# Two spectral-filter and MLP layers on one core: contiguous copies behind the d transform, a table half by DMA, and new instruction orders

## The chip, the core and the metric

The kernel runs on one core of a Trainium2 chip. The metric is the device time of one execution in microseconds (us). Of the kernel before there are three timed runs, with a median of 349.98 us (349.18 to 350.13), and one profiled execution, which took 349.9 us and whose instructions span 348.0 us. Positions in time below are microseconds from the start of that span.

## The reference

Two pairs of sublayers act on x, 2048 rows of 512 values in bf16 (2D transforms over both axes in FP32):

```python
x = x + irfft2(rfft2(layernorm(x)) * (w_r + 1j * w_i))      # A, a spectral filter
x = x + B(layernorm(x))                                     # B, an MLP with shifted rows
x = x + irfft2(rfft2(layernorm(x)) * (w_r + 1j * w_i))
x = x + B(layernorm(x))
```

B computes `h = gelu(layernorm(x) @ w1)`, shifts the four column quarters of h by -1, +1, -2 and +2 rows, multiplies by w2 and adds x (giving x1), and then returns `x1 + gelu(layernorm(x1) @ w3) @ w4`, with 1792 columns between w3 and w4. Both layers use the same weights.

## The kernel before

**Data.** x stays in SBUF as `K.x`, 128 partitions by 16 row slots q by 512 columns. Row number is 16p + q, so the transform over the 2048 rows splits into one over p (a matmul over the partitions) and one over q with twiddle factors.

**The stages of a layer**, with the letter that stands for each piece of work in the order strings:

- The first norm and the p transform. `s`, `i` and `J` compute mean and reciprocal deviation of a row slot; `Q` multiplies the table T of cosines and sines with the reciprocal deviation (`scaled_T`, L371 to L378, on DVE or ACT), and `O` is the matmul of x with that scaled table (L389, L391). So the norm costs no pass over x. `G` copies the products from PSUM to V (`take_V`, L416). In layer 1 this is `first_front` with the string ORDER_0; slots 1 and 5 have their sums made by ACT, and `FILL` puts two or three dummy matmuls behind some products. In layer 2 it is spread through the end of layer 1's MLP.
- The d transform: `d` (L504, matmuls with the table FA), then `t`, which copies its product from PSUM to a bf16 tile TV (`take_d`, L508 to L516). A unit is one or two blocks b of 128 rows of V, so a copy has 512 or 1024 columns. In layer 1 the copy permutes two halves h into alternate places; in layer 2 it is plain, since there the weights W have been permuted instead (`L`, L751).
- The q transform: `q` (L528, with the tables TL), `x` copies to X (L534), `p` multiplies X with W on DVE (`weigh`, L547). `b` is the q transform backwards (L558, with TR), `m` copies to hT (L569). The table TR has three planes, of which the third is the negated first.
- `D` and `P`: d and p transforms backwards (L576, L588); `Y` copies between them; `a` adds into x (L596).
- The MLP: `s`, `r`, `n` a norm, `T` a transposing DMA, `v` and `h` w1 and gelu, `u` w2 (L644), `f` and `E` the residuals, `k`, `R`, `o`, `U` the second norm and its transposes, `w` and `g` w3 and gelu (L679, L686), `W` w4 (L699, 14 matmuls of 512 columns), `A` the last residual (L705), `y` the store (L708). In layer 1, `W14` and `W24` are the two column halves of one row slot's product (`columns`, L688).

**What sets the order.** Nothing is scheduled at run time: ORDER_0, ORDER_A (layer 1) and ORDER_B (layer 2) list the work, each engine takes its own part of the list in that order, and waits for other engines arise from the data. A last letter V or A puts a copy on DVE or ACT, and a number behind a point names the PSUM bank. `X4.6` is four dummy matmuls. `WAKE` (L788) is the number of dummy matmuls at the very start.

**Loads.** SP's queue loads x in eight pieces and W in 16. POOL's queue (`load_rest`, L179) loads FA, TL and the first half of TR, and then, in this order, doubles W onto the odd partitions in four DMAs from SBUF to SBUF and makes the second plane of TL by two instructions for each half (`turn_TL`, L227: L230 and L231), then loads the second half of TR:

```python
double(0)
turn_TL(K, slice(0, 8))
double(1)
turn_TL(K, slice(8, 16))
double(2)
double(3)
load_TR(1)
```

`load_TR` fetches planes 0 and 1. The negated plane is made by DVE in two halves, `N0` and `N1` (`negate`, L759, L762). A DMA on SP (`gate2`, L201) reads W's last doubled row, so G, Tinv and w1 to w4, which stand behind it on SP, start when the doubling is done.

## Time and profile before

| | us | of the span of 348.0 |
|---|---|---|
| PE matmuls, 2129 | 339.1 | 97% |
| DVE | 185.6 | 53% |
| ACT | 197.2 | 57% |
| POOL | 61.8 | 18% |
| w3 products, L679, 448 | 99.8 | |
| w4 products, L699, 462 | 99.3 | |
| dummy matmuls, L254, 67 | 11.3 | |

Busy time of PE is the union of its matmuls, each counted from its start to its modelled end; they overlap, and 14 matmuls of 512 columns in a row take 3.02 us, 0.216 each, although each one's own duration is shown as 379 ns. The distance between two starts is therefore what counts in a row of matmuls, and dummy matmuls count as busy. The same holds on DVE and ACT in a smaller way: a following instruction starts up to 0.1 us before the one ahead of it ends, so a row of instructions takes less than the sum of their durations. A line of a group names line, engine, operation, what is written and read, and the shape, then total busy time, mean duration in ns, and the idle time of the engine just ahead of it with what ended it.

The first product of scaled tables starts at 8.46, the first d at 19.12, the first D at 39.18, the first v at 53.73, the first w at 82.16; in layer 2 the first d at 184.90, the first D at 204.57 and the first v at 219.24. The last matmul starts at about 343.7, the last add runs from 343.89 to 344.58, and its store lands at 346.38.

### The profile page before, as it was taken

To read this page: it belongs to the slowest core of one execution; us is meant where nothing else is said; L and a number is where in the kernel's file an instruction comes from. 1 tells how busy PE (TensorE), PEld (TensorE's weight loads), DVE (VectorE), ACT (ScalarE), POOL (GpSimd) and SP (SyncE) were. 2 spreads that over 40 slices of the span, in tenths; PEclk is the share of its full clock that TensorE was granted. 3 is DMA by queue.
4 is the path that set the end of the run, shared out by engine and by line. 5 is a ranking of instruction groups with operands and counts; after the bars stand their busy time and mean duration, and the time that the engine had idled before them with its cause. 6 is when DMAs were issued, how large, how long until landed. Compare 5 with 4: busy or idle time off the path is not lost. (4 is left out here: it accounts for less than half of the span.)

```text
span 348.0 us, 5581 instructions
## 1 busy us (share of the span) xinstructions
PE 339.1 (97%) x2129; PEld 189.3 (54%) x2129; DVE 185.6 (53%) x444; ACT 197.2 (57%) x350; POOL 61.8 (18%) x157
## 2 busy tenths in 40 slices
PE   8899999999999999999999999999999999999995
PEld 6778885444444444445577888544444444444442
DVE  5989596559424317844786969767343201102011
ACT  5979899754803706424528989985580372150410
POOL 2560055422200003200100002463130010000000
PEclk9999999999999999999999999999999999999999
DMA  7987935304030110400000002454003400400201
GB/s 240 319 326 238 377 82 115 75 13 57 1 62 0 30 33 0 90 2 0 1 2 0 2 2 44 80 107 76 0 2 60 90 0 16 107 0 17 75 0 60
DMA packets 45129, 24.38 MB, mean 70 GB/s; under 512 B 34928, under 2 KB 42096, under 8 KB 45104
## 3 DMA queue, kind: packets, MB, share of 16 engines
q1 hardware_dynamic: 43760, 20.00, 23.3%
q0 software_dynamic: 1104, 3.94, 3.0%
q8 instruction: 16, 0.26, 0.3%
q10 hardware_dynamic: 240, 0.10, 0.1%
q14 instruction: 9, 0.07, 0.1%
HBM read 11.41 MB, written 2.10 MB: 39 GB/s over the span
## 5 line engine op out<-in xcount | busy, mean ns | idle before, releaser
L686 ACT ACTIVATE gT<-ps 128x1024 bf16<-128x1024 f32 x56 | 56.4, 1022 | 103.6 <-PE ps L679 103.2
L679 PE MATMUL ps<-xT,w 128*128 128x512 bf16 x448 | 99.8, 379 | 0.5 <-DMA xT<-xn 0.5
L699 PE MATMUL ps<-w,gT 128*128 128x512 bf16 (+1 forms) x462 | 99.3, 373 | 0.0
L705 DVE TENSOR_TENSOR x_state<-ps,x_state 128x512 bf16<-128x512 f32 (+1 forms) x33 | 22.0, 674 | 98.0 <-PE ps L699 98.0
L699 PEld LDWEIGHTS <-gT 128*128 128x128 bf16 x462 | 45.1, 98 | 51.3
L679 PEld LDWEIGHTS <-w 128*128 128x128 bf16 x448 | 43.7, 98 | 53.1 <-DMA xT<-xn 0.9
L652 DVE SCALAR_TENSOR_TENSOR xn<-xn,ln_c,ps 128x512 bf16<-128x512 bf16 x32 | 23.3, 744 | 25.0 <-PE ps L644 9.3
L644 PE MATMUL ps<-w,hT 128*128 128x512 bf16 x128 | 29.3, 379 | 0.0
L628 PE MATMUL ps<-xT,w 128*128 128x512 bf16 x128 | 28.7, 379 | 0.0
L596 DVE SCALAR_TENSOR_TENSOR x_state<-ps,x_state 128x512 bf16<-128x512 f32 x32 | 20.4, 685 | 7.1 <-PE ps L588 7.0
L282 ACT ACTIVATE junk<-xn 128x512 bf16<-128x512 bf16 x32 | 19.9, 622 | 5.9 <-DVE xn L652 5.7
L270 DVE BATCH_NORM_STATS2 ln_st<-x_state 128x6 f32<-128x512 bf16 (+1 forms) x31 | 20.1, 667 | 3.5 <-DMA x_state<-in_A_x_dram 3.2
L644 PEld LDWEIGHTS <-hT 128*128 128x128 bf16 x128 | 12.4, 98 | 15.4 <-ACT hT L635 0.4
L628 PEld LDWEIGHTS <-w 128*128 128x128 bf16 x128 | 12.4, 98 | 14.9 <-issue 0.7
L282 ACT ACTIVATE xn<-x_state 128x512 bf16<-128x512 bf16 x32 | 20.0, 630 | 0.4
L547 DVE TENSOR_TENSOR PB<-X,W 128x2048 bf16<-128x2048 bf16 (+1 forms) x20 | 19.4, 1009 | 0.5 <-ACT X L151 0.4
L635 ACT ACTIVATE hT<-ps 128x512 bf16<-128x512 f32 x32 | 17.6, 605 | 3.2 <-PE ps L628 2.9
L288 POOL TENSOR_SCALAR ln_mv<-ln_s 128x4 f32<-128x4 f32 x16 | 4.3, 268 | 77.4 <-DVE x_state L596 66.7
L151 ACT ACTIVATE TV<-ps 128x1024 bf16<-128x1024 f32 (+1 forms) x15 | 14.3, 980 | 3.4 <-PE ps L504 2.1
L504 PE MATMUL ps<-FA,V 128*128 128x256 bf16 x128 | 16.0, 273 | 0.2 <-ACT V L151 0.2
L576 PE MATMUL ps<-G,hT 128*128 128x256 bf16 x128 | 15.3, 273 | 0.8 <-ACT hT L151 0.4
L305 POOL TENSOR_SCALAR ln_ve<-ln_mv 128x4 f32<-128x4 f32 x11 | 3.3, 298 | 71.8 <-DVE ln_mv L298 71.1
(86 smaller groups left out, 393.6 us busy)
## 6 DMA issues: line engine op xcount, KB each, us to landing
w<-in_B_w_dram SPq DMA_DIRECT2D x2, 1792.0 KB, 12.2
W<-W POOLq DMA_DIRECT2D x4, 514.0 KB, 4.7
x_state<-in_A_x_dram SPq DMA_DIRECT2D x8, 256.0 KB, 5.5
out_dram<-x_state SPq DMA_DIRECT2D x16, 128.0 KB, 1.9
TR<-tab_TR POOLq DMA_DIRECT2D x2, 512.0 KB, 6.4
w<-in_B_w_dram SPq DMA_DIRECT2D x2, 512.0 KB, 4.6
W<-in_A_w_r_dram SPq DMA_DIRECT2D x7, 128.5 KB, 6.1
W<-in_A_w_i_dram SPq DMA_DIRECT2D x7, 128.5 KB, 6.0
```

The lines of the kernel that those rows point to most:

```text
L270: self.K.nc.vector.bn_stats(self.st[i][:, int(k)], src)
L282: K.nc.scalar.activation(out, src, ACT.Square, bias=0.0, scale=D ** -0.5, accum_out=self.s[:, i, 1:2])
L547: nc.vector.tensor_tensor(t, X.pop(u)[:, 0:2 * n].unsqueeze(1).to_broadcast([P, 2, 2 * n, 256]), K.W[:, :, 2 * u:2 * u + 2 * n, 1:257], op ...
L596: nc.vector.scalar_tensor_tensor(K.x[:, q, :], ps.pop(("P", q)), 1.0, K.x[:, q, :], op0=ALU.mult, op1=ALU.add, accum_out=ln[g].s[:, i, 0:1])
L628: nc.tensor.matmul(o[:, i], lhsT=K.w1[:, t, j * P:(j + 1) * P], rhs=xT[g][:, :, t, :], start=(t == 0), stop=(t == 3))
L635: nc.scalar.activation(hv[:, 2 * h + i, 4 * g:4 * g + 4, PAD:PAD + P], o[:, i].rearrange("p (q c) -> p q c", q=4), ACT.Gelu_apprx_tanh, bi ...
L644: nc.tensor.matmul(o, lhsT=K.hT[:, j, st:st + P], rhs=K.w2[:, j, :], start=(j == 0), stop=(j == 3))
L652: nc.vector.scalar_tensor_tensor(xn[:, q, :], xn[:, q, :], ln[q // 4].c[:, q % 4:q % 4 + 1], ps.pop(("u", n)), op0=ALU.mult, op1=ALU.add, ...
L679: nc.tensor.matmul(o[:, i], lhsT=K.w3[:, c, t * P:(t + 1) * P], rhs=xT3[g][:, :, c, :], start=(c == 0), stop=(c == 3))
L686: nc.scalar.activation(gT[g][:, 2 * j:2 * j + 2, :], ps.pop(("w", k)), ACT.Gelu_apprx_tanh, bias=0.0, scale=1.0)
L699: nc.tensor.matmul(o, lhsT=gT[g][:, t, i * P:(i + 1) * P], rhs=K.w4[:, t, d], start=(t == 0), stop=(t == 13))
L705: nc.vector.tensor_tensor(x, ps.pop(("W", n)), x, op=ALU.add)
```

## The change

- `take_d` in layer 1 writes TV contiguously and reads PSUM with the two halves h innermost: consecutive elements lie 128 FP32 apart, in pairs. The same values go to the same places as before; only the order in which the copy walks over them differs.
- The table TR in DRAM gets its negated plane. The first half is loaded as before, two planes, with `N0` making the third on DVE; the second half is loaded with all three planes, and `N1` is gone.
- Behind the first doubling of W, POOL copies two values of the last scaled table of the first norm into a tile `gate` that nobody reads, and so waits for that table there.
- 35 dummy matmuls at the start instead of 44.
- In layer 2 row slot 10 of the list is made in two column halves (`W10`, `W20`), each with its own add and its own store, as row 14 was in layer 1 (where this stays).
- All three orders are new. ORDER_0 begins with rows 0 and 1 and puts Q0, Q1 and Q9 on DVE, Q8 on ACT. In layer 1 the TV copies on ACT are 0, 1, 4, 8, 10, 12 and 15 (before 1, 2, 8, 10 and 12), and of the hT copies 1, 2, 3, 6, 7 and 9 are on DVE (before 0, 1, 8 and 9), half of 15 in both. In layer 2 the TV copies 1, 8 and 15 go to DVE, where ACT made all before, and x4 goes to ACT. Counts of matmuls, copies and products are otherwise as they were.

The diff, with the long orders cut to their starts, layer 1's first MLP part and their ends:

```diff
--- before.py
+++ after.py
@@ -88,6 +88,7 @@
     Bt = B.transpose(0, 1, 3, 2)
     TR = np.stack([np.stack([At, Bt], axis=3), np.stack([Bt, -At], axis=3)], axis=2)
     TR = TR.reshape(NH, 2, 2, 32, 2, 64).transpose(3, 2, 1, 4, 0, 5).reshape(P, 2, NH, 64)
+    TR = np.concatenate([TR, -TR[:, :1]], axis=1)
     out = {"T": np.stack([T, -T], axis=1), "FA": FA, "TL": TL, "TR": TR, "G": G, "G2": G2,
            "Tinv": np.stack([T.T, -T.T], axis=1)}
     return {k: np.ascontiguousarray(v.astype(ml_dtypes.bfloat16)) for k, v in out.items()}
@@ -176,16 +177,18 @@
     K.TL = K.const.tile([P, 2, NB, P], BF16, name="TL")
     K.TR = K.const.tile([P, 3, NH, 64], BF16, name="TR")
 
-    def load_rest():
+    def load_rest(after):
         q = nc.gpsimd
         load_TL = lambda k: q.dma_start(K.TL[:, 0, 8 * k:8 * k + 8], dram["TL"][:, 8 * k:8 * k + 8])
-        load_TR = lambda k: q.dma_start(K.TR[:, 0:2, 16 * k:16 * k + 16], dram["TR"][:, :, 16 * k:16 * k + 16])
+        load_TR = lambda k: q.dma_start(K.TR[:, 0:2 + k, 16 * k:16 * k + 16], dram["TR"][:, 0:2 + k, 16 * k:16 * k + 16])
         double = lambda k: q.dma_start(K.W[1::2, :, 8 * k:8 * k + 8], K.W[0::2, :, 8 * k:8 * k + 8])
         table("FA", q)
         load_TL(0)
         load_TL(1)
         load_TR(0)
         double(0)
+        gate = K.const.tile([1, 2], BF16, name="gate")
+        q.tensor_copy(gate[:], after[0:1, 0, 0:2])
         turn_TL(K, slice(0, 8))
         double(1)
         turn_TL(K, slice(8, 16))
@@ -438,6 +441,8 @@
             L[g].sums()
     ps = {}
 
+    last_T = None
+
     def stats(q):
         g, i = at[q]
         if q in ON_ACT:
@@ -451,8 +456,10 @@
         L[g].aggr(i)
 
     def scale(q, eng):
+        nonlocal last_T
         g, i = at[q]
         scaled_T(K, q, L[g].r[:, i:i + 1], eng)
+        last_T = K.Tq[q]
 
     def front(k):
         ps[k] = over_p(K, FIRST[k], k == len(FIRST) - 1)
@@ -474,7 +481,7 @@
             table[op[0]](int(op[1:-1]), op[-1])
         else:
             table[op[0]](int(op[1:]))
-    K.load_rest()
+    K.load_rest(last_T[:])
     K.load_mlp()
     spare = K.grp.tile([P, 4, 4, P], BF16, name="xT", bufs=4)
     K.nc.sync.dma_start_transpose(spare[:, 0, 0:1], K.zeros[:])
@@ -512,8 +519,8 @@
         if last:
             copy(K, tv[u][:], src, eng)
         else:
-            copy(K, tv[u][:].rearrange("p n (e f h) -> p (n e) h f", e=2, h=2),
-                 src.rearrange("p n (e h f) -> p (n e) h f", e=2, h=2), eng)
+            copy(K, tv[u][:].rearrange("p n (e f h) -> p (n e) f h", e=2, h=2),
+                 src.rearrange("p n (e h f) -> p (n e) f h", e=2, h=2), eng)
 
     def over_q(u):
         bs = UNITS[u]
@@ -687,9 +694,9 @@
 
     def columns(n):
 
-        if last or n % 10 != 4 or n < 14:
+        if n not in (HALVES[last], HALVES[last] + 10):
             return n, slice(0, D)
-        return 14, slice(0, D // 2) if n == 14 else slice(D // 2, D)
+        return HALVES[last], slice(0, D // 2) if n == HALVES[last] else slice(D // 2, D)
 
     def w4(n):
         r, d = columns(n)
@@ -705,7 +712,8 @@
         nc.vector.tensor_tensor(x, ps.pop(("W", n)), x, op=ALU.add)
 
     def store(n):
-        nc.sync.dma_start(K.out_v[:, ROWS[n], :], K.x[:, ROWS[n], :])
+        r, d = columns(n)
+        nc.sync.dma_start(K.out_v[:, ROWS[r], d], K.x[:, ROWS[r], d])
 
     def stats4(n):
         r, d = columns(n)
@@ -785,13 +793,14 @@
             table[op[0]](int(op[1:]))
 
 
-WAKE = 44
+WAKE = 35
 FILL = {0: 3, 1: 3, 2: 2, 3: 2, 4: 2}
 GROUPS = [[0, 1, 2, 3], [4, 5, 6, 7], [8, 9, 10, 11], [12, 13], [14, 15]]
 ON_ACT = [1, 5]
 FIRST = [[0, 1], [2, 3], [4, 5], [6, 7], [8, 9], [10, 11], [12, 13], [14], [15]]
 UNITS = {b: [b, b + 1] if 2 <= b < 14 else [b] for b in (0, 1, 2, 4, 6, 8, 10, 12, 14, 15)}
 ROOT = (0, 1)
+HALVES = (14, 10)
 LATE = ((14, 15), (0, 14))
 TAKE_B = ("FFFFFFFFFFFFFFFB", "FFFFFFFFFFFFFFFB")
 ROWS = [*range(2, 16), 0, 1]
@@ -799,46 +808,46 @@
 PLAIN = 5
 FLEX = "mGnotxY"
 ORDER_0 = """
-s0 s2 s3 i0 i2 i3 s1 f0 S0 s4 J0 Q2V Q3V O1 i4 s5 s7 s6 Q1A Q0A i7 i6 G1A f1 S1 O0 G0A s11 s10 i11 J1 Q6A i10 s8 s9
-Q7A Q4A i8 i9 s13 Q5A s12 S2 J2 i13 i12 Q10V O3 G3A Q11A O2 Q8V O5 Q9A s15 s14 S3 J3 i15 i14 G2A S4 Q13V Q12V J4 Q14V
-G5A Q15A O4 O6 G6A G4V O7 G7V O8 G8A G8V
+s0 s2 i0 s3 s1 i2 i3 f0 s4 S0 J0 i4 s5 Q1V Q0V Q3V Q2V s7 s6 i7 i6 s9 s11 O0 G0A f1 i9 S1 J1 s8 O1 G1A Q6A s10 Q7A i11
+O3 i8 i10 Q5A s13 s12 Q4A O2 S2 J2 i13 Q10V G3A i12 Q9V s15 Q11A O5 S3 Q8A s14 i15 G2A O4 i14 S4 J3 Q12V G5A J4 Q15A
+Q13V O6 Q14V G6A G4V O7 G7V O8 G8V G8A
 """
 ORDER_A = """
-N0 X4.6 d0.5 t0V d1.7 t1A d2.2 t2A q0.0 x0V p0 q1.6 d4.4 d10.0 q2.2 x1A t10A p1 t4V d6.6 t6V q4.4 x2A x4A p2 p4 d12.1
-t12A q10.6 q6.3 d14.0 d8.1 t14V x6A p6 x10A b0.3 t8A b3.5 b2.6 m2A b5.4 b1.0 p10 m3A m1V m0V m5A q8.1 x8A q12.6 N1
-d15.5 t15V b6.0 b4.3 b7.2 x12A q15.6 m4A p8 p12 q14.4 m6A x14A b10.3 b9.0 m10A m9V b11.1 m7A x15A p14 p15 m11A b8.4
-b12.5 m12A b13.0 m13A m8V b14.1 m14A b15.6 m15V m15A D1.3 Y1A D0.0 Y0A D3.5 Y3A P2.3 a2 s2 P3.1 P0.0 a3 s3 a0 s0 P1.2
...
-T1 v0.6 r2 v1.3 s15 c2 h0 a13 h1 T2 a12 n9V T3 v3.5 s12 n8V T4 h3 n11V v2.3 u0.0 h2 s13 u1.4 n10V s14 r3 c3 u3.5 f1 T5
-k1 v5.3 h5 f3 k3 v4.1 h4 f0 n15V n13V n12V u2.7 n14V f2 T6 k0 u6.6 f6 u4.1 E1 E2 k2 k6 f4 T7 u7.4 u5.0 f5 v7.1 h7 R0
-E3 o3A f7 v6.0 u8.3 f8 o2V h6 u11.4 o1A E4 u9.0 u15.5 E0 o0V f15 u13.3 k8 f9 f13 k9 f11 u10.1 k5 L15 E7 E5 k4 u12.2 E6
-k7 R1 U1 f10 k11 o6V f12 u14.3 U0 L13 w3.4 w6.6 g6 L4 w1.1 g1 g3 o5V f14 k10 w0.6 w2.0 g2 g0 L12 w5.2 g5 o7V o4A E8
...
-W12.7 L7 j11 j9 O3.5 W15.4 j8 A12 B12 G3A G3V A15 B15 S2 Q10 z0 j15 S15 Q8 J15 j12 W13.2 Q15 W24.5 Q9 W14.3 A13 B13
-j13 S13 S12 Q11 A24 J13 Q13 O4.0 G4A J12 B24 Q12 A14 B14 j14 S14 O15.6 G15V G15A J14 Q14 O5.4 G5A O6.2 G4V O14.6 G14V
-G6A G14A X4.5 X3.4 L6
+X4.1 N0 d0.3 t0A d2.5 d1.7 t1A d4.0 t4A q0.2 x0A t2V q1.4 x1V p1 d10.6 d6.4 p0 t6V q2.1 t10A q4.6 x2A p2 x4A d12.3
+b1.0 q6.1 p4 q10.6 t12A m1V b3.3 m3V x6A d8.4 d14.2 d15.0 x10A b5.6 t8A q8.4 p6 t14V t15A q12.0 b2.7 p10 m2V q14.2 m5A
+x8A x12A q15.4 b0.6 m0A b10.7 m10A b4.1 m4A p8 b6.0 p12 m6V x14A p14 b11.7 x15A b9.1 p15 b13.6 m11A m9V m13A b7.3
+b12.5 m12A b8.2 m8A b14.7 m14A m7V b15.5 m15A m15V D1.1 Y1V D0.5 D3.3 P2.7 a2 P3.2 a3 Y0A P0.1 a0 Y3A P7.4 P1.7 a1 s2
...
+L0 v0.1 h0 a12 a13 v1.5 h1 T3 r2 c2 v3.4 n11V s12 c0 n10V T5 n8V n9V h3 s15 v2.3 h2 u0.5 L8 u3.0 u2.7 f0 L2 s14 f3
+u1.5 f1 s13 r3 n12V n14V n15V f2 T4 v5.2 n13V h5 v4.1 u4.5 f4 E1 h4 u7.6 u6.1 f7 E3 u5.4 T7 k1 k0 f6 f5 k3 k2 E5 R0 c3
+T6 v7.5 h7 u15.7 E0 v6.0 h6 E6 E4 u8.4 k7 o0V k5 o1V f15 E2 k6 o2V u10.3 o3V f10 k10 u12.7 u11.0 f8 u14.1 f14 U0 U1
+u9.2 f9 k9 k8 w2.4 g2 f12 L9 E9 k4 R1 f11 k11 R2 w5.6 E11 g5 w4.2 g4 w1.0 u13.4 E8 o8V g1 o9V w3.5 g3 f13 E10 o10V
...
+Q10 G1V g27 W12.5 A12 O3.0 B12 W15.6 j12 Q5 G3A G3V A15 O2.2 G2A B15 Q8 j15 G2V S15 J15 Q15 W13.5 A13 B13 S12 W24.4
+A24 j13 S13 J12 Q12 B24 J13 W14.5 Q13 A14 B14 O4.0 G4A O15.2 j14 S14 O5.6 G15V G15A O6.4 J14 Q14 O14.2 G4V G5A X3.7
+G14V L6 G6A X4.1 G14A
 """
 ORDER_B = """
-d4.0 d1.3 d8.6 t4A q4.0 t1A q1.2 t8A x4V d15.5 t15A p4 d12.6 x1A p1 t12A d10.4 q15.0 x15A p15 t10A q8.2 x8V q12.6 x12A
-d2.0 t2A d0.4 d14.5 b1.3 m1A q10.0 t0A q2.6 t14A p8 b8.3 x2A m8A d6.4 t6A p12 x10V b5.2 m5A p2 b12.1 m12A p10 b13.0
-q0.4 m13V q6.6 x0A x6A q14.2 b4.1 m4A p0 b10.4 b11.5 p6 x14A m11A m10A b3.6 m3A b9.0 b0.1 m0A p14 m9V b7.2 m7V b2.7
...
-W5.0 A5 y13 w20.5 W7.4 g20 w14.2 g14 A7 w15.4 y4 g15 w16.0 g16 w18.5 g18 W9.2 A9 y7 W8.3 A8 W11.4 y15 A11 W10.7 A10 y5
-y6 y14 y11 y9 y8 y10
+d1.1 d4.3 t1V d15.7 t15V d8.0 t8V t4A q1.2 x1A p1 q4.6 x4A p4 d12.4 q15.2 t12A d10.6 x15A p15 t10A q8.0 q12.4 x12A
+b1.2 m1A d14.6 d2.3 t14A x8V p12 t2A d0.0 t0A b5.2 m5A p8 q10.5 x10V p10 q2.3 x2A d6.0 t6A b9.2 p2 b4.3 m9A q0.4 x0A
+p0 q14.6 m4A x14A q6.0 x6A b13.2 b12.4 m12A b10.3 b0.7 m0A p14 b3.5 m3A b2.0 m13A m10V p6 b14.3 b11.4 m2V b8.6 m11A
...
+W6.4 A6 w14.0 w15.3 g15 W5.2 g14 w18.0 A4 A5 g18 w17.6 g17 y7 y5 y6 w19.4 g19 W9.2 A9 W10.5 y4 y9 A10 y10 W8.0 A8
+W11.4 W20.6 A11 A20 y8 y14 y11 y20 z0
 """
```

## The prediction

> **What bounds the kernel now.** I read the page's busy shares first: PE is busy for 97% of the span, so a gain must come from places where PE runs dummy matmuls, waits, or has ended. To find them I cut the span at the borders of the stages:
>
> ```profile
> core 0: us, PE busy (x) PEld busy (x) DVE busy (x) ACT busy (x) POOL busy (x), PEclk, DMA share, GB/s
> 1.01:8.46 7.45, 7.45 (x44) 5.66 (x45) 4.24 (x13) 5.05 (x13) 1.73 (x9) 1.00 0.85 267
> 8.46:19.12 10.66, 9.35 (x82) 7.58 (x79) 10.27 (x31) 9.62 (x19) 5.97 (x8) 1.00 1.00 334
> 19.12:39.18 20.06, 19.50 (x256) 15.88 (x257) 18.38 (x24) 18.08 (x26) 4.65 (x6) 1.00 0.85 298
> ...
> 82.16:184.90 102.74, 102.51 (x533) 50.36 (x533) 56.42 (x144) 43.60 (x63) 10.92 (x22) 1.00 0.09 19
> 184.90:204.57 19.67, 19.00 (x256) 16.31 (x257) 16.53 (x20) 18.22 (x29) 0.00 (x0) 1.00 0.01 2
> ...
> 219.24:343.87 124.63, 124.61 (x578) 56.09 (x575) 38.26 (x96) 54.29 (x95) 19.96 (x52) 1.00 0.20 46
> 343.87:348.00 4.13, 0.00 (x0) 0.00 (x0) 0.69 (x1) 0.00 (x0) 0.00 (x0) 0.97 0.10 33
> ```
>
> The two long stretches after 82.16 and 219.24 are matmul back to back; nothing can be won there. The stretch to 8.46 is 44 dummies. From 8.46 to 19.12 DVE is busy for 10.27 of 10.66 us: the first norm is bound by DVE. The spectral stage of layer 1 (19.12 to 39.18) has 256 matmuls. PE's timeline starts 64 of them 0.109 us apart (d), 64 in pairs at 0.055 each (q), 128 at 0.056 (b), so PE needs 17.6 of 20.06 us, while DVE (18.38) and ACT (18.08) are nearly full. That stage is bound by copies, in layer 1 with dearer ones than in layer 2. First ACT in layer 1 (window 18.6 to 39.5), then the same group in layer 2 (184 to 206):
>
> ```profile
> L151 ACT ACTIVATE X<-ps 128x1024 bf16<-128x1024 f32 x6 | 5.9, 1048 | 0.0
> L151 ACT ACTIVATE TV<-ps 128x1024 bf16<-128x1024 f32 x4 | 5.3, 1328 | 0.8 <-PE ps L504 0.6
> ```
>
> ```profile
> L151 ACT ACTIVATE TV<-ps 128x1024 bf16<-128x1024 f32 x6 | 6.2, 1035 | 1.2 <-issue 1.2
> ```
>
> Layer 1's copy writes every second bf16 and costs 1.328 us; layer 2's, contiguous, 1.035. On DVE in layer 1:
>
> ```profile
> L149 DVE CAST TV<-ps 128x1024 bf16<-128x1024 f32 x2 | 2.6, 1308 | 0.2 <-PE ps L504 0.2
> L149 DVE CAST TV<-ps 128x512 bf16<-128x512 f32 x3 | 2.2, 735 | 0.2 <-PE ps L504 0.2
> L762 DVE TENSOR_SCALAR TR<-TR 128x1024 bf16<-128x1024 bf16 x2 | 0.9, 457 | 0.0
> ```
>
> DVE's contiguous cast of that size (X in layer 2) takes 1.222. PE's own waits are short, so a small loss is enough to make new ones:
>
> ```profile
> PE ps L389 <- DMA W<-in_A_w_i_dram: 1.2, 1, 1.2
> ...
> PE ps L679 <- DMA xT<-xn: 0.5, 1, 0.5
> PE ps L576 <- ACT hT L151: 0.4, 1, 0.4
> ```
>
> The first (at 11 to 12.2) is really a wait for a scaled table of ACT: Q6A starts at 11.66 and O3 at 12.21, and O3 reads no W. Last, DVE's timeline where the first norm meets POOL's turning of TL, which begins at 15.67:
>
> ```profile
> 13.80 0.47 DVE L376 TENSOR_SCALAR Tq<-T,ln_r 128x256 bf16<-128x256 bf16 x2
> ...
> 15.73 0.82 DVE L376 TENSOR_SCALAR Tq<-T,ln_r 128x256 bf16<-128x256 bf16 x2
> ```
>
> The same two instructions take 0.47 us alone and 0.82 beside POOL.
>
> [...]The new read takes each element [...](neighbours 512 bytes apart); the trace shows no such read, so this stays a risk. Against it: take_V jumps after every four elements[...] and still costs 1.02 us for 1024 on ACT. On SBUF writes [...]a step of 4 bytes costs 28% on ACT.
>
> **The change part by part.**
>
> *First norm (ORDER_0, WAKE, gate).* Nine dummies fewer: the last of them run 0.109 us apart, so they end at 8.46 - 0.98 = 7.48. Q1 and Q0 now stand on DVE ahead of Q3 and Q2, so O0 can start when DVE has done them, about 7.6. This is not the gain: the end of the stage is DVE's. DVE takes two scaled tables more (2 x 0.19 start to start, +0.38) and ACT two fewer. The gate puts POOL's turning behind the last scaled table: Q12/Q13 go back to 0.47 (-0.35) and Q14 (0.59 at 16.82) to 0.27 (-0.3). DVE's idle pieces before J1 (0.22), s4 (0.19) and Q14 (0.1) shrink by some 0.2. Sum -0.45: the first d at about 18.7 instead of 19.12. What the gate queues behind it on POOL: two turns (1.66 + 0.77, 1.79 + 0.75), three doublings of W and TR's second half. From a gate at 16.6 the first turn ends at 19.2 (q0 reads it at 21.4), the second at 22.5 (q10 reads it at 26.7). The last doubling waited for W until 23.51 before and still does, so SP's gate2 with G, Tinv and w1 to w4 behind it keeps its time: cost 0.
>
> *Negation by DMA.* N1 goes: one DVE instruction, 0.42 (0.33 start to start). TR's second half grows from 512 to 768 KB. It was issued at 24.12 and landed at 29.44; 256 KB at the stage's 298 GB/s are 0.9, so 30.3. b10 is now the sixth b, but its p10 ends on DVE at about 31.9: slack 1.5. SP's weights share the engines and may land up to 0.9 later; w4 then lands at 47.0, ahead of the first xT transpose (48.99 before, about 48 now). Cost 0; at most 0.5 if the transposes are caught behind them.
>
> *The copies behind d.* Unknown price of the pair read. Lower end: the contiguous price, 1.035 on ACT and 1.222 on DVE[...]. Upper end: [...]On ACT 512 columns cost 0.61 and 1024 1.035, so 1024 stream in 0.84 and would cost 1.87; on DVE (0.69, 1.22) 2.28. I take the lower end, since the four-element runs of take_V show no price for jumps.
>
> *Layer 1's spectral stage.* DVE start to start is a weigh 1.14 (small 0.60), a hT copy 0.60 (half 0.38), a strided TV 1.21 (small 0.64), contiguous 1.13 (0.61). Before, from the first weigh at 22.33: ten weighs 9.24, two big and two small TV 3.70, four and a half hT 2.78, N1 0.33: 16.05, measured 16.67 to the last hT at 39.00, so 0.6 of waits. After: weighs 9.24, one big and one small TV 1.74, six and a half hT 3.98: 14.96. The first weigh, p1, now waits for x1 on DVE itself: d0 18.7, d2, d1, d4, q0, q1 end at 21.95, x1V 22.15, p1 22.75. ACT loses 2.0: its seven TV cost 4 x 1.035 + 3 x 0.61 = 5.97, where five strided ones cost 4 x 1.328 + 0.741 = 6.05 (-0.1); it gives away two hT copies (-1.3), and I let the other nine and a half come down from this stage's 0.70 to layer 2's 0.635 (-0.6). With ACT lighter I halve the waits: 22.75 + 14.96 + 0.3 = 38.0, and the first D 0.2 later at 38.2, against 39.18: **-1.0**, the -0.45 of the norm included.
>
> *MLP of layer 1.* Before PE waited at 81.5 to 82.16 (0.63) for U0's transpose, which landed at 82.02. In the new order seven u and two v stand between R0 and the first w, 9.5 us, against eight u and one v, 8.6; all four o of group 0 go to DVE. That wait should vanish: -0.6. In return u3 follows u0 directly behind v2, and h2's second half ends some 0.3 after PE wants it: +0.3. Sum **-0.3**. The other moves (o8 to o11 and o15 from ACT to DVE, o13 and o14 to ACT, the permutations, z0) fall into 82.16 to 184.90, where DVE is busy for 56 and ACT for 44 of 103 us behind PE: 0.
>
> *Layer 2.* DVE idled 2.34 us at 185.6 waiting for a q. The order fills that with t1, t15 and t8 and moves x4 to ACT; behind x8 DVE's list is as long as before, and x8 ends 0.25 earlier by the same durations. The 0.46 wait for Y0 (on DVE behind four adds) goes as Y0 goes to ACT, but other waits of this kind will come: **-0.3** for both. The move from layer to layer (180.67 to 184.90) is the chain A14, B14, j14, S14, J14, Q14, O14, G14 in both: 0.
>
> *End.* Row 10's last product is split in halves: 28 matmuls at 0.109 for 14 at 0.216, +0.03. The last add is 256 wide (0.42, row A24's size) instead of 0.69; its store was issued 0.03 after the add and landed 1.77 later. **-0.27**; two halves add one store on SP, issued during the last matmuls.
>
> Sum: -1.0 - 0.3 - 0.3 - 0.27 = -1.9 on a span of 348.0, so 346.1. The profiled run took 349.9, beside a median of 349.98, so 348.1 is the forecast.
>
> **Rivals.** *Hidden or given back.* The pair read costs what the strided write did, 1.33, or new waits (U1 before the first w of layer 2 is due within 0.2 us of its use; T6 in layer 1 within 0.4) eat the rest. ACT then gains 0.4 rather than 2.0 and the stage ends near 38.9; with the end and half of the MLP's -0.3 that is about 349.3. For it: ACT's and DVE's loads are equal, so either can hold PE. Against it: N1 and DVE's TV are gone in any case.
>
> *Slower[...].* One mechanism: the pair read at half rate. In layer 1 ACT copies 5632 columns (+4.6 us) and DVE 2560 (+2.7). ACT had 18.08 busy in 20.06; 16.1 + 4.6 with 2 us of starts and gaps gives 22.7, so the first D comes 2.6 later, less the 0.45: about +2.2 instead of -1.0, and with the other -0.87 a time of 351.3. It decides from about 1.5 us for a 1024 copy on ACT, where the stage's loss equals the rest's gain. [...]Against it: the jumps in take_V.
>
> **Numbers.** Forecast case, 346.4 to 348.9: 0.63. Hidden, 348.9 to 350.9: 0.20. Slower: 0.17. A measurement of this kernel tells about 0.3%, 1.05 us, from no change, so faster is under 348.9; the first case and a small part of the second give 0.66, same 0.17, slower 0.17. The range runs from 346.4 to 350.6.
>
> **What would show it.** In the profile after: the layer-1 TV row on ACT at 1.03 (right) or over 1.4 (wrong); Tq pairs on DVE all near 0.47; the first L504 near 18.7 and the first L576 near 38.2; TR's second landing before 31; no wait at the first L679; a last DVE add of 0.42. The forecast is wrong above all if the pair read is dear, or if DVE waits for X or V in the new order.

## The result, and the profile after

The changed kernel takes **348.3 us** (median of 6 runs, 348.06 to 348.41) beside 350.08 of the kernel before on the same chip: a ratio of 0.9951, 95% interval 0.9938 to 0.9964. Its profiled execution took 348.26 and spans 346.5 us, against 348.0 before. So 1.5 us of the span have gone, and 1.8 between the medians; 1.9 were forecast. The lines of the code have moved down by 1 to 8: the d, q, backward q, D and P products stand at L511, L535, L565, L583 and L595, v, u, w and W at L635, L651, L686 and L706, the copies at L150 (DVE) and L152 (ACT), `N0` at L770, the last add at L712.

The span cut at the same borders as before (columns as there):

```profile
core 0: us, PE busy (x) PEld busy (x) DVE busy (x) ACT busy (x) POOL busy (x), PEclk, DMA share, GB/s
7.50:18.64 11.14, 9.61 (x83) 7.70 (x81) 10.95 (x36) 10.13 (x20) 5.80 (x11) 1.00 0.96 314
18.64:38.38 19.74, 19.25 (x259) 16.18 (x256) 17.88 (x23) 17.44 (x26) 5.41 (x7) 1.00 0.86 289
38.38:53.09 14.71, 14.47 (x128) 12.43 (x128) 12.36 (x35) 12.49 (x30) 3.81 (x13) 1.00 0.80 214
...
183.49:203.07 19.58, 19.17 (x256) 15.97 (x256) 18.02 (x22) 17.23 (x27) 0.00 (x0) 1.00 0.01 2
203.07:218.37 15.30, 14.51 (x128) 12.44 (x128) 11.11 (x33) 14.24 (x32) 4.48 (x15) 1.00 0.24 46
218.37:343.04 124.67, 124.16 (x581) 57.58 (x590) 36.49 (x93) 54.84 (x95) 19.14 (x48) 1.00 0.20 44
343.04:346.50 3.46, 0.00 (x0) 0.00 (x0) 0.42 (x1) 0.00 (x0) 0.00 (x0) 1.00 0.18 57
```

The lengths of the stages set beside those before give the account of the 1.5 us. The starts are those of the first weight load of each kind of product.

| stretch | before | after | difference | forecast |
|---|---|---|---|---|
| start to first d | 19.12 | 18.64 | -0.48 | -0.45 |
| first d to first D, layer 1 | 20.06 | 19.74 | -0.32 | -0.55 |
| first D to first v, layer 1 | 14.44 | 14.71 | +0.27 | 0 |
| first v to layer 2's first d | 131.28 | 130.40 | -0.88 | -0.3 |
| first d to first D, layer 2 | 19.64 | 19.58 | -0.06 | -0.3 with the next |
| first D to first v, layer 2 | 14.59 | 15.30 | +0.71 | |
| MLP of layer 2, to the last matmul | 124.72 | 124.67 | -0.05 | 0 |
| from there to the end | 4.14 | 3.46 | -0.68 | -0.27 |

So two stretches grew, each of them the one that ends at a first v. The copies behind d in layer 1 (groups of the window 18.4 to 39.5):

```profile
L152 ACT ACTIVATE TV<-ps 128x1024 bf16<-128x1024 f32 x4 | 4.2, 1038 | 0.3 <-PE ps L511 0.3
L150 DVE CAST TV<-ps 128x1024 bf16<-128x1024 f32 x2 | 2.4, 1220 | 0.8 <-PE ps L511 0.8
L152 ACT ACTIVATE TV<-ps 128x512 bf16<-128x512 f32 x3 | 1.9, 617 | 1.6 <-PE ps L511 1.6
```

They cost 1.038 and 1.220 us beside contiguous copies of 1.035 and 1.222 in layer 2 before, so the pair read from PSUM costs nothing more here. PE's waits:

```profile
PE ps L392 <- ACT Tq L381: 1.2, 1, 1.2
...
PE ps L635 <- DMA xT<-xn: 0.9, 2, 0.7
PE ps L583 <- DVE hT L150: 0.8, 2, 0.5
```

The wait of w (L679 before, L686 now) for its transpose is gone from PE's own lines, as forecast. A new one has come at v (L635): twice, 0.15 in layer 1 and 0.74 in layer 2, where it is the longest that the change has brought:

```profile
218.40 1.89 PE L635 MATMUL ps<-xT,w 128*128 128x512 bf16 x8 [0.74 <-DMA xT<-xn]
```

DVE's timeline around the borders:

```profile
16.04 0.48 DVE L379 TENSOR_SCALAR Tq<-T,ln_r 128x256 bf16<-128x256 bf16 x2
...
18.68 0.79 DVE L770 TENSOR_SCALAR TR<-TR 128x1024 bf16<-128x1024 bf16 x1
...
22.84 1.30 DVE L554 TENSOR_TENSOR PB<-X,W 128x1024 bf16<-128x1024 bf16 x2
...
36.60 1.66 DVE L150 CAST hT<-ps 128x512 bf16<-128x512 f32 x3
...
343.08 0.42 DVE L712 TENSOR_TENSOR x_state<-ps,x_state 128x256 bf16<-128x256 f32 x1 [0.84 <-PE ps L706]
```

The scaled pair is back at 0.48. `N0`, 0.49 before (at 19.22), now takes 0.79, since POOL's turning runs beside it instead: its copy L234 from 18.43 to 19.18, with `N0` from 18.68 to 19.47. (Where the turning comes earlier, in the run without the gate, `N0` takes 0.42.) The first weigh (22.84) and the end of the last hT copy (38.26) come 0.1 and 0.3 later than in the sum, 22.75 and 38.0. The last add is 0.42.

### The profile page after: what moved, and what is told of

Read it like the earlier page. It is cut to its first block, busy times and chain, and to the rows that moved or that the text cites. A ratio compares the mean times of both kernels' runs of the same rounds, so it can differ in the third digit from the quotient of the medians.

```text
span 346.5 us, 5563 instructions
## 1 busy us (share of the span) xinstructions
PE 337.5 (97%) x2116; PEld 190.0 (55%) x2134; DVE 187.9 (54%) x452; ACT 192.0 (55%) x342; POOL 65.2 (19%) x158
## 4 chain that ended last, share of the span: by engine, by line
PE 80%; DVE 8%; ACT 5%; DMA 4%; issue 2%; DVEq 0%; SPq 0%; ACTq 0%
PE ps L686 28%; PE ps L706 27%; PE ps L635 8%; PE ps L651 8%; PE ps L511 3%; DVE x_state L603 3%; DMA xT<-xn 2%; ACT V L152 2%; PE ps L583 2%; DVE PB L554 2%; PE ps L535 1%; DMA x_state<-in_A_x_dram 1%; DVE hT L150 1%; ACT X L152 1%; DMA T<-tab_T 1%
## 5 line engine op out<-in xcount | busy, mean ns | idle before, releaser
L686 PE MATMUL ps<-xT,w 128*128 128x512 bf16 x448 | 99.3, 379 | 0.1
L706 PE MATMUL ps<-w,gT 128*128 128x512 bf16 (+1 forms) x464 | 97.8, 366 | 0.6
L712 DVE TENSOR_TENSOR x_state<-ps,x_state 128x512 bf16<-128x512 f32 (+1 forms) x34 | 22.1, 657 | 108.6 <-PE ps L706 106.9
L706 PEld LDWEIGHTS <-gT 128*128 128x128 bf16 x476 | 46.5, 98 | 49.9
L686 PEld LDWEIGHTS <-w 128*128 128x128 bf16 x448 | 43.7, 98 | 52.9 <-DMA xT<-xn 0.6
L635 PE MATMUL ps<-xT,w 128*128 128x512 bf16 x128 | 28.8, 379 | 0.9 <-DMA xT<-xn 0.9
L651 PE MATMUL ps<-w,hT 128*128 128x512 bf16 x122 | 28.6, 379 | 0.3
L635 PEld LDWEIGHTS <-w 128*128 128x128 bf16 x128 | 12.4, 98 | 16.0 <-issue 1.6
L651 PEld LDWEIGHTS <-hT 128*128 128x128 bf16 x128 | 12.5, 98 | 15.1
L293 POOL TENSOR_TENSOR ln_mv<-ln_s,ln_t 128x4 f32<-128x4 f32 x16 | 3.5, 217 | 75.4 <-ACT junk L285 70.0
L583 PE MATMUL ps<-G,hT 128*128 128x256 bf16 x128 | 15.4, 272 | 0.9 <-DVE hT L150 0.8
L565 PE MATMUL ps<-TR,PB 128*128 128x128 bf16 x256 | 16.1, 219 | 0.1
L565 PEld LDWEIGHTS <-PB 128*128 128x128 bf16 x256 | 14.8, 98 | 1.5 <-issue 1.2
```

Of the source, the lines that this page charges most:

```text
L565: nc.tensor.matmul(oh, lhsT=pab[u][:, k, 2 * (b - u) + h, F * P:(F + 1) * P], rhs=K.TR[:, k:k + 2, 2 * b + h], start=(k == 0), stop=(k == 1))
L583: nc.tensor.matmul(o[:, i, e * 256:(e + 1) * 256], lhsT=M[:, F, e, 2 * m + i, :], rhs=K.G[:, F, e, :], start=(F == 0 and e == 0), stop=(F ...
L635: nc.tensor.matmul(o[:, i], lhsT=K.w1[:, t, j * P:(j + 1) * P], rhs=xT[g][:, :, t, :], start=(t == 0), stop=(t == 3))
L651: nc.tensor.matmul(o, lhsT=K.hT[:, j, st:st + P], rhs=K.w2[:, j, :], start=(j == 0), stop=(j == 3))
L686: nc.tensor.matmul(o[:, i], lhsT=K.w3[:, c, t * P:(t + 1) * P], rhs=xT3[g][:, :, c, :], start=(c == 0), stop=(c == 3))
L706: nc.tensor.matmul(o, lhsT=gT[g][:, t, i * P:(i + 1) * P], rhs=K.w4[:, t, d], start=(t == 0), stop=(t == 13))
```

## The experiments

Ratios are to the kernel before on the same chip, with their 95% intervals. Two profiles of one and the same program (the last experiment repeats the changed kernel) differ by 0.2 us in the start of the first d, 18.64 and 18.44, but agree on the stretch from there to the first D, 19.74 in both. So starts in the first stages are read to 0.2 us, lengths more finely. The kernel before scatters as much: with the same first norm its first d is at 19.12 and, in the run with the new copy alone, at 19.34.

### The old copy in the new orders

```diff
-            copy(K, tv[u][:].rearrange("p n (e f h) -> p (n e) f h", e=2, h=2),
-                 src.rearrange("p n (e h f) -> p (n e) f h", e=2, h=2), eng)
+            copy(K, tv[u][:].rearrange("p n (e f h) -> p (n e) h f", e=2, h=2),
+                 src.rearrange("p n (e h f) -> p (n e) h f", e=2, h=2), eng)
```

> The changed kernel with the old copy behind layer 1's d transform (alternate bf16 written, PSUM read in a row); all else as changed. Theory (this stage is bound by copies): TV rows go back to 1.33 us on ACT and 1.31 on DVE for 1024 columns, so ACT gets 4 x 0.29 + 3 x 0.13 = 1.5 us more and DVE 0.2; the first D moves from 38.38 to 39.0 to 39.5, and the time from 348.3 to 348.9 to 349.4. Rival (the new orders alone moved the stage, the copies had slack): first D within 0.2 of 38.4 and a time of 348.2 to 348.5.

Measured: 348.93 us, ratio 0.9978 (0.997 to 0.9986). The groups of the same window:

```profile
L152 ACT ACTIVATE TV<-ps 128x1024 bf16<-128x1024 f32 x4 | 5.3, 1334 | 0.1
L150 DVE CAST TV<-ps 128x1024 bf16<-128x1024 f32 x2 | 2.6, 1299 | 0.8 <-PE ps L511 0.8
```

ACT pays 0.296 more for each large copy and DVE 0.079. From the first d (18.68) to the first D (39.04) it is 20.36 instead of 19.74: the new walk is worth **0.62 us** in the new orders. In the window from first d to first D ACT's busy time rises by 1.24 (18.68 against 17.44) and DVE's by 0.27; the stage pays something between, which fits two lists that hold PE by turns. With the old copy the new orders are slower here than the old ones (20.36 against 20.06, and that without `N1`): they pay only together with the new copy.

### The new copy alone, in the kernel before

The same edit the other way round, in the kernel before.

> The kernel before with nothing but the new copy behind layer 1's d transform. Theory (bound by copies): TV at 1.04 us on ACT and 1.22 on DVE; ACT loses 1.3 us and DVE 0.3, and as DVE's list was the longer one the first D comes 0.3 to 0.6 earlier than 39.18, time 349.5 to 349.8 beside 350.1 before. Rival (pairs of reads are only cheap where the order leaves room, or only the orders gain): first D within 0.15 of 39.18 and time within 0.2 of before.

Measured: 349.53, ratio 0.999 (0.9981 to 0.9999).

```profile
L151 ACT ACTIVATE TV<-ps 128x1024 bf16<-128x1024 f32 x4 | 4.1, 1022 | 1.2 <-PE ps L504 1.2
L149 DVE CAST TV<-ps 128x1024 bf16<-128x1024 f32 x2 | 2.4, 1220 | 0.4 <-PE ps L504 0.4
```

The copies are as cheap as in the changed kernel, yet first d to first D is 19.82 instead of 20.06, 0.24 less. (The first D itself, at 39.16, has hardly moved, since in this profile the first d came 0.22 later.) In the old order ACT's saving goes into waits, 1.2 us ahead of these copies. What is gained is near what DVE itself saves on its five TV copies, 0.09 at each of the two large and 0.05 at each of the three small ones. The cheaper copy gives its whole worth only with the work divided anew.

### Without the gate

```diff
-        gate = K.const.tile([1, 2], BF16, name="gate")
-        q.tensor_copy(gate[:], after[0:1, 0, 0:2])
```

> The changed kernel without POOL's copy that waits for the last scaled table; POOL turns TL as soon as the first doubling is issued. Theory (the end of the first norm is DVE's, and POOL's turning lengthens scaled tables there): pairs of scaled tables beside POOL take about 0.8 us again rather than 0.48, the first d comes 0.3 to 0.6 later than 18.64, and the time is 0.2 to 0.6 above 348.3. Rival (the scaled tables are short, and what DVE loses is absorbed behind them; the turning earlier even helps N0, 0.79 in the changed kernel): first d within 0.15 and a time of 348.0 to 348.4.

Measured: 348.65, ratio 0.9964 (0.9952 to 0.9976). DVE's timeline without the gate, where POOL's turning runs from 15.37:

```profile
16.06 1.05 DVE L377 TENSOR_SCALAR Tq<-T,ln_r 128x256 bf16<-128x256 bf16 x2
16.44 1.22 DVE L150 CAST V<-ps 128x1024 bf16<-128x1024 f32 x1
17.96 1.02 DVE L150 CAST V<-ps 128x512 bf16<-128x512 f32 x2 [0.30 <-PE ps L392]
18.90 0.42 DVE L768 TENSOR_SCALAR TR<-TR 128x1024 bf16<-128x1024 bf16 x1
```

The pair goes from 0.48 to 1.05, and `N0` from 0.79 to 0.42. So POOL's turning does hold an instruction of DVE, but not every one: the turn of 1.66 us covers three scaled tables, of which the first takes 0.38 instead of 0.29, the second its usual 0.26, and only the last is held, for 0.87, until the turn has ended. Nor does DVE's list get longer by that. The copy of V behind the held table starts at 16.44, 0.67 us before that has ended where 0.1 is usual (with the gate at 16.43), and is done at 17.66 in both. What comes later is the product that reads this table; the next copy waits 0.30 for it and starts at 17.96 instead of 17.74. And the longer `N0` of the changed kernel costs nothing there, as DVE idles 0.78 us behind it.

The first d starts at 18.76, 0.1 and 0.3 later than in the two profiles of the changed kernel. Counted from DVE's first scaled table, which takes out when x arrives, the first d comes after 11.46 us here, and after 11.29 to 11.31 in all ten profiles of the changed order that have the gate and no dummies added behind a product. So the gate is worth 0.17 us, by one profile without it. The times can't show that, as the two ratios overlap; of the expectation, the first d fits the rival and the time the theory.

### Row 10 in one piece

```diff
-HALVES = (14, 10)
+HALVES = (14, 99)
```

and `W10 A10 y10` in place of the two halves at the end of the order.

> The changed kernel with row 10 of layer 2 in one piece again (one product of 512 columns, one add, one store, still last). Theory as in the prediction: only the add is longer, 0.69 instead of 0.42, so the time goes up by 0.27, to 348.6. Rival: the smaller store and what comes behind it carry the rest of the 0.67 us that the traces show between the last matmul and the end, so the time goes up by 0.5 to 0.7, to 348.8 to 349.0, with the store's landing 0.2 longer.

Measured: 348.73, ratio 0.9971 (0.9959 to 0.9983). In this profile x landed about 1 us late, so its span isn't comparable, but its end is: from the end of the last matmul (343.97) to the end of the span (347.93) it is 3.96 us, against 3.46. The last add takes 0.69 instead of 0.42, and the last store lands 1.77 us after its issue, like the whole row's before, where the half lands after 1.55. The split is worth 0.27 + 0.22 = **0.49 us**, as the rival had it. The other 0.2 of the end's 0.68 lies between the last landing and the end of the span, 1.61 before and 1.43 here, where nothing is split: it belongs to something else, which stayed open.

### The dummies at the start

```diff
-WAKE = 35
+WAKE = 44
```

> The changed kernel with 44 dummy matmuls at the start as before. Theory (the end of the first norm is DVE's list, PE's start is not): the first product of the norm comes at 8.5 instead of 7.6, but the first d within 0.2 of 18.64, and the time is 348.1 to 348.5; as PE's instruction packets move by nine matmuls, the first transposes of layer 1 may land earlier, which can make it up to 0.3 faster. Rival (PE's later start is carried through by the copies of V): first d 0.5 to 0.9 later, time 348.8 to 349.1.

Measured: 348.71, ratio 0.9969 (0.9958 to 0.9981), an interval that overlaps the changed kernel's. In the profile the first d is at 18.47 and the first D at 38.21, no later than without the nine dummies. But this profile doesn't hold the case that was to be tested: its first product starts at 7.82, not at 8.5, and in the changed kernel at 7.87 and, in the repetition, 7.69. The first dummies of every profile start 0.21 us apart and the later ones 0.109, and where the step between them falls differs from run to run: at about 5.0 here, 6.3 before, 6.5 in the changed kernel. The last of 35 dummies starts anywhere from 6.31 to 7.50 in nine profiles, the last of 44 at 7.71 here. What an earlier first product is worth is thus not shown by this run. That DVE's list ends the stage is borne out in another way, by the fixed 11.29 to 11.31 us from its first scaled table to the first d.

### The negated plane by DVE again

TR's second half as two planes, and `N1` behind `p10`.

> The changed kernel with TR's second half loaded as two planes and its negation made by DVE again, right behind the weigh of block 10. Theory: DVE's list gets 0.33 us longer in the stage that it binds, so the first D comes 0.2 to 0.5 later and the time is 348.5 to 348.8; the load is 256 KB smaller, TR lands about 1 us earlier than 30.7 and w4 0.5 to 1 us earlier than 46.8, without use for the first D. Rival (DVE has that slack, and the 256 KB cost as much as they save): time 348.1 to 348.4.

Measured: 348.62, ratio 0.9974 (0.9961 to 0.9986). First d to first D is 20.03 instead of 19.74: `N1` on DVE costs 0.29, about its own 0.33. The loads end 1 us earlier (the spare transpose behind w4 lands at 46.15 instead of 47.14), and yet layer 1's T0 takes 4.7 us, as in the changed kernel. So the transposes are not late because w4 is. (A later run shows the converse: there the spare transpose lands at 47.48, and T0 takes 3.1.)

### An earlier start of layer 1's order

ORDER_A begins with

```
X4.1 N0 d0.0 t0A d1.1 t1A d2.2 t2V q0.4 x0A q1.6 x1A p0 p1 d4.0 t4A q2.2 x2A d6.4 t6V q4.6 x4A p2 d10.0 t10A ...
```

that is, with units 0 and 1 first and their X on ACT.

> The changed kernel with only the start of layer 1's list in another order: d0 d1 d2 q0 q1 ahead of d4, x1 on ACT instead of DVE, q2 ahead of d6 and d10, some banks changed for it. DVE idles 0.78 and 0.63 us there in the changed kernel and the first weigh starts at 22.84. Theory (behind the first weigh the stage is DVE's list): the first weigh starts near 21.8, the first D 0.6 to 1.1 earlier than 38.38, and the time is 347.3 to 347.9, a part of the gain being lost to the xT transposes that wait for w4 and for instruction packets. Rival (PE or ACT, which gets x1, or W's doublings then hold the stage): first D within 0.3 of 38.38 and time 348.0 to 348.5.

Measured: 348.29, ratio 0.9964 (0.9956 to 0.9972), the changed kernel's time. DVE's timeline:

```profile
21.83 1.78 DVE L554 TENSOR_TENSOR PB<-X,W 128x1024 bf16<-128x1024 bf16 x2
...
28.11 0.69 DVE L150 CAST hT<-ps 128x512 bf16<-128x512 f32 x1 [0.34 <-ACT X L152]
...
36.46 1.65 DVE L150 CAST hT<-ps 128x512 bf16<-128x512 f32 x3
```

The first weigh starts 1.01 us earlier than in the changed kernel (21.83 against 22.84), the last hT copy ends 0.15 earlier. The second small weigh waits for ACT's X (two that take 1.30 together are spread over 1.78), and so does a copy at 28.11 (0.34). So the rival came true: with DVE's start relieved, ACT's copies are the next bound, and the two lists are balanced to some tenths of a us. What the first D gained (38.22 instead of 38.38) is lost again ahead of the first v, where T0 takes 5.0 us.

### Thirteen more dummies

`FILL[1]` 13 instead of 3, and `X7.1` instead of `X4.1`, in layer 1 only. This was to move a DMA packet that had turned up in the lists of DMA packets, of the kind "instruction", away from the transposes.

> The changed kernel with 13 more dummy matmuls, ten behind the second product of the first norm (PE idles there for 1.2 us) and three ahead of layer 1's first d (0.4 us idle). They use idle time, but move every later 16 KB packet of the instruction queue 13 matmuls earlier in PE's program. In the changed kernel one such packet (49.73, 0.95 us long) lies inside the first xT transposes of layer 1, which land 4.6 and 3.5 us after their issue instead of 3.1 to 3.3, and PE waits for them ahead of the first v. Theory (the packet delays the transpose): the packet comes near 48.3, the first transpose lands within 3.9 us of its issue, the wait of PE for xT there is gone, and the time is 0.2 to 0.5 under the changed kernel's, 347.8 to 348.1. Rival (the transpose is late because w4, landing at 46.8, and the transpose of zeros behind it hold the queue): still 4.4 to 4.8 us, wait and time as in the changed kernel (348.2 to 348.4).

Measured: 348.7, ratio 0.997 (0.9958 to 0.9982): no gain. The packet moved only from 49.73 to 48.60, still behind T0's issue (47.81), and T0 took 4.2 us. Four later transposes, at about 94 and 231, took 4.0 to 5.1, each with such a packet in its time. Nor did the dummies only use idle time: the first d comes 11.62 us behind DVE's first scaled table instead of 11.29. The expectation failed; the theory was not yet refuted, since the packet had not been moved out of the way.

### Moving the instruction packets further

On PE, 26 of the dummies at the start each cut in two, which adds 52 PE instructions and no PE time:

```diff
-    fill(K, WAKE)
+    for i in range(52):
+        nc.tensor.matmul(K.ps[:, 7 if K.bank is None else K.bank, 0:128], lhsT=t[:], rhs=t[:], start=True, stop=True)
+    fill(K, WAKE - 26)
```

> The changed kernel with 26 of the first 35 dummies on PE each cut into two of half the width: the same PE time, 52 instructions more (26 weight loads and 26 matmuls). In layer 1 of the changed kernel T0 and T1 take 4.6 and 3.5 us and PE waits 0.9 us for xT, while a 16 KB packet of the kind 'instruction' on queue 8 lies at 49.73, inside T0's data; these packets come about every 256 PE instructions, before the change at 48.48, ahead of the data. Theory: it brings PE's instructions and delays the transposes. Then 52 instructions move it some 2 us earlier, to about 47.7; T0 takes 3.2 to 3.6 and T1 3.1, and the first v starts 0.4 to 0.7 earlier than 53.09. What that is worth at the end is less sure, since the other packets move too and may meet other transposes. Rival: T0's lateness belongs to what stands ahead of it on its queue: T0 still takes 4.5 or more with the packet gone from its data. Layer 2's T3 stays at 3.8 by both.

Measured: 348.12, ratio 0.9957 (0.9943 to 0.9972). The DMA view of 47 to 53.5 in 40 slices, first of the changed kernel, then of this one:

```profile
DMA  0000000000069999999900990007999994004999
GB/s 0 0 0 0 0 0 0 0 0 0 0 134 230 219 202 202 321 173 174 11 0 0 52 22 9 9 9 147 285 298 176 285 295 75 0 0 98 219 216 214
...
q8 instruction: 1, 0.02, 0.9%
```

```profile
DMA  0000000005999999920029999999400000399999
GB/s 0 0 0 0 0 0 0 0 0 104 227 217 213 214 202 197 196 45 0 0 50 213 219 213 216 208 206 196 92 2 0 0 0 0 66 221 217 206 213 216
```

In the second no instruction packet starts in the window: T0's data moves in one piece from 48.5 to 49.9, then T1's and T2's. In the first the packet falls into the first burst (the slice of 321 GB/s), and behind it lies a hole of some 1.3 us with 0 to 52 GB/s, before the rest of T0 and T1 moves. So T0 takes 3.1 us instead of 4.6, T1 3.1 instead of 3.5, and PE's timeline has no wait ahead of the first v:

```profile
50.32 2.35 PE L597 MATMUL ps<-Y,Tinv 128*128 128x256 bf16 x20
52.51 1.67 PE L637 MATMUL ps<-xT,w 128*128 128x512 bf16 x7
```

First D to first v is 14.32 us (38.08 to 52.40) instead of 14.71. (Of the 0.9 us of waiting that the expectation puts ahead of layer 1's first v, 0.15 are there and 0.74 in layer 2. The rest of the gain in layer 1 is that v's start now overlaps the end of P.) The profiled runs of layer 1's T0, by the time from its issue to the packet of queue 8 next to it:

| run | T0 issued | packet | packet after issue | T0 took | T1 took |
|---|---|---|---|---|---|
| 52 PE instructions more | 47.29 | 45.62 | -1.7 | 3.1 | 3.1 |
| before | 48.99 | 48.48 | -0.5 | 3.3 | 3.1 |
| 13 dummies more | 47.81 | 48.60 | +0.8 | 4.2 | 3.3 |
| changed kernel | 47.59 | 49.73 | +2.1 | 4.6 | 3.5 |
| changed kernel again | 47.40 | 50.25 | +2.9 | 4.9 | 3.8 |

A packet half a us or more ahead of the issue does nothing here; one 0.8 to 2.9 us behind it costs 1 to 1.9 us. The other runs agree: in the seven other profiles of the changed order with the packet 2.0 to 2.9 us behind the issue, T0 takes 4.5 to 5.0, and in the kernel before with the new copy alone (packet at -0.5) 3.3. What happens to the data can be seen in the changed kernel: the transpose's packets of 256 bytes, 18 ns long as a rule, take 0.65 to 1.4 us where they start between 50.0 and 50.8, while the instruction packet (49.73 to 50.68) is under way and just behind it. The late T0 of layer 1 is thereby explained and shown. The gain is not kept: two transposes about 93 us now take 4.9 and 4.3 (there was a packet at 95.77), layer 2's first v is 0.40 earlier than in the changed kernel's repetition, and in time the kernel can't be told from the changed one.

The same on ACT: eight one-column copies more, in layer 1's MLP.

```diff
+        if n == 8 and not last:
+            nudge = K.const.tile([P, 1], FP32, name="nudge")
+            for _ in range(8):
+                nc.scalar.activation(nudge[:], K.eps[:], ACT.Copy, bias=0.0, scale=1.0)
```

> The changed kernel with eight one-column copies more on ACT, in the middle of layer 1's MLP where ACT idles. In layer 2 of the changed kernel the first v waits 0.74 us for transpose T3 (issue 214.45, landed 218.27, 3.8 us where most take 3.1 to 3.2), and the DMA records show an 8 KB packet of the kind 'instruction' on queue 14 at 216.94, inside T3's data; before, that packet came at 212.4 and no transpose there took over 3.3. Theory: the packet brings ACT's instructions and delays T3. Then eight instructions more on ACT bring it some 4 us earlier, to about 212 to 214, T3 takes 3.1 to 3.2, the first v starts at about 217.7 instead of 218.37, and the time falls by up to 0.7 us, 0.2%. Rival: the packet is another engine's, or a mere neighbour: it stays within 0.5 us of 216.9 or moves while T3 stays at 3.8, and the first v at 218.4. Layer 1 is the same by both.

Measured: 348.23, ratio 0.9953 (0.9941 to 0.9965). The theory fell: the packet of queue 14 stays at 216.96, T3 at 3.8 us, the first v at 218.53. Eight ACT instructions more moved it by 0.02 us, so it doesn't follow their number. Whether it delays layer 2's T3 was not settled, though the runs allow it: T3 takes 3.8 to 3.9 in all twelve runs of the new orders, with the packet some 2.5 us behind its issue, and none of layer 2's transposes took over 3.3 in the two runs of the old order, where it comes at about 212. What the trace does show is that T3's data isn't late. Its last packet is through at 217.08, 2.6 us after the issue as usual; the landing comes 1.2 us after that instead of 0.5 to 0.7. Against the packet speaks that the transpose issued at 223.01 has one of queue 14 just as far behind it (2.4 us) and takes 3.2.

Both edits together:

> Both edits at once. Theory: both waits go, first v of layer 1 at about 52.5, of layer 2 at about 217.0 (against 218.37), time about 347.0 to 347.5 beside 348.3 of the changed kernel: the best version. Rival: one or both waits stay, and the time is that of the changed kernel, 348.3 within 0.4.

Measured: 348.14, ratio 0.9947 (0.9935 to 0.9959). In this profile the loads came late: `N0` waited 1.57 us for TR's first half (landed at 20.03 instead of 17.99), the first D began at 39.4, and w4 landed only at 50.19, behind T0's issue (48.58), while a packet of queue 8 lasted from 47.44 to 50.77; T0 took 4.1, and either can be the reason. Of the expectation it shows nothing. And the changed kernel once more, on the same chip:

> The changed kernel itself once more, on the same chip as the three others, so that their ratios to the kernel before can be set against its own: 0.9951 was measured, 0.994 to 0.997 is expected here, with T0 at 4.6, T3 at 3.8 and the first v of layer 2 at 218.4, if these are fixed by the program (by both theories).

Measured: 348.34, ratio 0.9963 (0.9949 to 0.9977), T0 4.9, T3 3.8, layer 2's first v at 218.41. None of the variants is shown to beat the changed kernel.

## Why the prediction was right, and where its terms were not

**The time** (348.1 forecast, 348.3 measured) and the sign were right, and the likeliest case is the one that came. That the sum is so close is in part luck: of the span, layer 2, the stretch of D and P and layer 1's spectral stage gave 1.45 us less than forecast, and the MLP of layer 1 and the end 0.99 more, part of both for reasons that were not in the forecast. Point by point:

- **First norm, -0.45.** Measured -0.48 in the profile after and -0.68 in its repetition, with a scatter of 0.2 on both sides. That DVE's list ends the stage was right. That the earlier first product is not the gain fits this, but was not tested. Where the dummies end was forecast from their number alone, which does not fix it. The gate's part, taken as -0.35 and -0.3, was too large: it gives 0.17, because DVE's next instruction, the copy of V, started 0.67 us before the held table had ended. What is left of the -0.48 would be the new order of DVE's list; that was not run alone.
- **The pair read at the contiguous price.** Right: 1.038 and 1.220 forecast as 1.035 and 1.222. The slower rival, the half-rate read, is refuted. Its price, 1.87 us on ACT and 2.28 on DVE, was the author's estimate: the streaming part of a copy taken twice, which no trace had shown. A walk whose neighbours are 512 bytes apart costs ACT and DVE nothing here. The old copy, which writes with a step of 4 bytes and reads in a row, costs ACT 0.296 and DVE 0.079 more for 1024 elements. As the jumping read with a contiguous write costs what a wholly contiguous copy does (1.038 beside 1.035 on ACT), the step on the write side is what the copy paid for.
- **Layer 1's spectral stage, -0.55 beyond the norm.** Measured -0.32. The mechanism was right: each taken back alone, the copy's walk is worth 0.62 and the negation by DMA 0.29, which was counted as one instruction of DVE's list (0.33). That is more than the 0.32 measured, since the new orders by themselves lose in this stage. DVE's list from the first weigh to the last hT copy took 15.42 us, forecast 14.96 + 0.3: it was 0.16 too short, its start 0.1 too early.
- **Negation by DMA, cost 0.** Right: TR's second half landed at 30.68 (forecast 30.3), w4 at 46.81 (47.0), and with the loads 1 us shorter T0 was as late.
- **D and P of layer 1, 0.** Mis-sized: +0.27. Transposes "caught behind" w4 were allowed for, at up to 0.5; they are caught by PE's instruction packet instead. With that packet out of the way the stretch is 14.32, under the 14.44 before.
- **MLP of layer 1, -0.3.** Measured -0.88. The U0 wait went (0.63 between the starts around it, forecast 0.6). The forecast took it for a matter of order alone. In the old kernel's trace U0's transpose was itself late: it took 3.8 us, with an instruction packet of queue 14 at 79.83, beside which its 256-byte packets, 18 ns as a rule, took up to 1.0 us. At the usual 3.1 to 3.2 it would have landed at 81.4, ahead of its use. In the new copy's run in the old orders that packet came earlier, U0 took 3.5, and the stretch from the first v to the first w was 0.24 shorter (28.27 against 28.51). In the new orders U0 lands 2.6 us before the first w. The given-back 0.3, u3 waiting for h2, did not come: PE's waits have none at L651. That term should have been 0. The last 0.25 lies in no single wait, and part of it is the border itself, since before the first v's weights were loaded while P still ran.
- **Layer 2, -0.3.** This is the term that failed, in sign too: +0.65. DVE's idle 2.34 us was indeed filled (0.69 remain), but first d to first D fell by only 0.06, so that idle had held nothing. And the new wait of 0.74 us for T3 ahead of the first v was not in the forecast; "other waits of this kind will come" named no size. T3 landed at 218.27 after 3.8 us instead of 3.1 to 3.2, so some 0.6 of it is lateness of that landing and the rest the norm ahead of it. Why it is late stays open.
- **End, -0.27.** The mechanism was right and the size too small: -0.68, of which 0.27 is the add, 0.22 the half store's earlier landing, left out of the sum, and 0.2 after the landing, not from the split.
- **The hidden rival** was wrong on the copy's price but right in kind: the stretches to the two first v grew by 0.27 and 0.71, mostly by waits for transposes in other places than those it named.

## What to carry to other kernels

Where an engine must permute on the way from PSUM to SBUF, let the read jump and write contiguously; here this took 22% off ACT's large copies (1.334 to 1.038 us) and 6% off DVE's (1.299 to 1.220). But a cheaper copy gives its worth only when the work is divided anew: alone it gave 0.24 us, in the new orders 0.62. And a transposing DMA that PE waits for with no slack is a risk in a tuned order, because its duration depended here on where instruction packets fell: issue it one to two us earlier than its usual duration demands (T0 took 3.1 to 5.0), and where two follow each other closely, expect the first to suffer more (4.6 and 3.5 for T0 and T1, 4.3 and 3.8 for the two transposes at 76.92 and 78.25 before).
